# A planner's costs for overlapping steps, half-width products in P V, and matmuls into unprimed banks, in a fused attention and two-MoE kernel

## The chip, the cores and the metric

The kernel runs on one core of a Trainium2 chip. The metric is device time in microseconds, the median over runs. Engine names below: PE is TensorE (PEld its weight loads), ACT is ScalarE, DVE is VectorE, POOL is GpSimd, SP is SyncE, whose queue issues most DMAs.

## The reference

Attention with a window of 32 keys and 32 global tokens, then two feed-forward blocks, all in fp32; 2304 tokens of width 512.

```python
B, H, S, D = 4, 8, 512 + 32, 64             # 512 local and 32 global tokens
s_g = scale * q_g @ concat(k_g, k_l).T      # global queries see every key
out_g = softmax(s_g) @ concat(v_g, v_l)
s_ll = where(abs(i - j) <= 32, scale * q_l @ k_l.T, -1e9)
out_l = softmax(concat(scale * q_l @ k_g.T, s_ll)) @ concat(v_g, v_l)
x = concat(out_g, out_l)                    # 2304 x 512
h = x @ w_in                                # 512 -> 2048
y = (h * clip(h + 3, 0, 6) / 6) @ w_out     # 2048 -> 512
z = maximum(maximum(y @ w1, y @ w2), y @ w3)    # 512 -> 768
out = z @ w_out2                            # 768 -> 512
```

## The kernel before

No instruction is issued where it is written. Every function calls `op(engine, us, fn, due, r=, w=)`, which records a step with an engine (or two to choose from: `AD` is ACT or DVE, `DP` is DVE or POOL), an assumed duration, a priority and the buffers that it reads and writes. At the end `Plan.order()` runs a list scheduler over all steps: for each engine it keeps the time at which it is free (`free`), takes the ready step of least `due`, and writes the order down; the engines then run their queues in that order on the chip, and semaphores hold what is not ready. The assumed durations are constants beside each `op` (0.665 for an exponential of 224 columns, 0.47 for a row maximum) or the functions `mmt`, `act`, `dve`, `pool` of the number of columns. In `order()` a step that depends on another engine's step may start 0.12 after that one's end, a PE step's result is there `DRAIN` after its last issue, and an engine is free at the end of its step. `rel` is an earliest planned time, which holds loads back; the loads of the later weights are released `LAG` before their use.

The stages in the order of time:

- Attention, 16 pairs of heads (`pair`), four to a batch. Per pair: scores (L421, four 64x64 tiles of the PE array), row maximum with the mask added (L434, DVE), exponential (L440, ACT), guard and reciprocal (DVE or ACT), normalization (L465, POOL), transposes `flip` (L477, PE), copies out of the bank (L379, ACT or DVE) and P V (`pv`, L503): for each of four blocks i of 128 queries, two blocks of keys (kb 0 with 128 rows, kb 1 with 96), each for both heads side by side in the array. The keys stand in the order global, first 256 local, global, and so on, so that each query block sees two key blocks. Global queries have their own steps (`globals_`, L536 to L577).
- The first product x @ w_in (`first`, L643), in between the attention steps as soon as its weights are decoded (`decode`, `join`: L590 to L617) and its tokens are there. Every fp32 operand is split in a high and a low part, and three matmuls stand for one product.
- The second product (`long_`, L807), the third (`quad`, L931) and the fourth (`single` L1087, `double`) by seven block products P1 to P7 where a plain split has eight, on token groups A (256 columns), B (512) and C (320). The operands come back from DRAM (`gload`, L796), are split (L730 on ACT, L625 on DVE), and sums of banks are copied from bank to bank (`take`) so that a later product accumulates on them.

The PSUM has eight banks. In the third and fourth products `quad` uses tag `bac` for the banks that a product starts afresh and `bb` for the one into which `take` copies a partial result, on which a matmul then accumulates without a start. For this, before the third product, `prime` runs one 128x512 matmul with a start into each of the two banks of `bb` (6 and 7).

The costs as they stand before:

```python
mmt = lambda n, cols: n * (cols + 32) / 2400.0
act = lambda n: 0.18 + n * 0.00083
dve = lambda n: 0.155 + n * 0.00104
pool = lambda n: 0.08 + n * 0.0025
```

Of the kernel before, what the change touches and what calls it, by code (L numbers as in the profile page):

```python
# [20 lines left out]
B, H, SL, SG, D = 4, 8, 512, 32, 64  # L21
# [75 lines left out]
class Plan:  # L97
# [39 lines left out]
    def order(self):  # L137
# [4 lines left out]
        free, cand, out, pipe, port, form = {}, {}, [], 0.0, 0.0, "F"  # L142
# [40 lines left out]
        while len(out) < len(self.ops):  # L183
            picks, wait, at = [], {}, {}
# [15 lines left out]
            t, _, _, _, o, e = min((p for p in picks if p[0] <= t0 + WAIT), key=lambda p: p[1:4])  # L200
# [13 lines left out]
                form = FORM.get(o.what, "F")  # L214
                o.us += TURN
            o.start, o.end = t, t + o.us
            free[o.eng] = o.end
            if o.two:
                port = o.end
            if o.kb:  # L220
# [6 lines left out]
            out.append(o)  # L227
            for s in o.succ:
                s.left -= 1
                s.ready = max(s.ready, o.end if s.eng == o.eng and not o.kb else o.done + 0.12)  # L230
                if not s.left:
                    enter(s)
        return out
# [2 lines left out]
PLAN = []  # L236
WAIT = 0.02
RATE = 340.0
DRAIN = 0.18
PAIRS = 3  # L240
SPLIT = 2
WIDE = 4
TS = "BC"
STEPS = (7.2, 13, 13, 15)
LAG = 84.0
W4DUE = 4
BIAS = -0.5
SHARE = 0.0
# [8 lines left out]
def body(ctx, tc, q_n, k_n, v_r, msk, msk_g, w_in, w_o, w_3, w_4, out):  # L257
    nc = tc.nc
# [3 lines left out]
    op = plan.op  # L262
    mmt = lambda n, cols: n * (cols + 32) / 2400.0
# [62 lines left out]
    ps = Region("ps", lambda at, n: banks[at])  # L326
# [14 lines left out]
    T = {}  # L341
# [46 lines left out]
    def pair(b, pr, s0):  # L388

        S = {}  # L390
# [14 lines left out]
        for grp in (((0, 1),) if b >= PAIRS else ((0,), (1,))):  # L405
# [89 lines left out]
            def pv(grp=grp):  # L495

                for u in grp:
                    for v in range(2):
                        i = 2 * u + v
                        for kb, n in ((0, 128), (1, 96)):  # L500
                            at = (2 * v + kb) * 128
                            for hh in range(2):
                                nc.tensor.matmul(ob()[64 * hh:64 * hh + 64, 128 * i:128 * i + 128],  # L503
                                                 lhsT=V()[0:n, hh, i + kb], rhs=PTS[u][hh]()[0:n, at:at + 128],
                                                 start=(kb == 0), stop=(kb == 1))

            op("PE", 0.92 * k, pv, s1 + 7, r=[x for u in grp for x in PTS[u]] + [V], w=[(ob, u) for u in grp], what="pv")

# [325 lines left out]
    plan.event(lambda: (p1.close(), rr.open(), rf.open()), ("lp", "rx", "rq"), ("rr", "rf"))  # L834
    t = TC
    for i, (p, c, seed) in enumerate(turns):
        if i == 2:
            WO["s"] = Buf(T["wb"])
            w_sum("s", "21", "22", ALU.add, TC + 2 * LEN - 12)
            w_long("P5", "s", TC + 2 * LEN - 4)  # L840
            w_sum("s", "s", "11", ALU.subtract, TC + 3 * LEN - 18)
            w_long("P6", "s", TC + 3 * LEN - 6)
            w_sum("21", "11", "21", ALU.subtract, TC + 3 * LEN - 14)
            w_long("P7", "21", TC + 4 * LEN - 8)
            w_long("P4", "22", TC + 5 * LEN - 8)
            w_sum("12", "12", "s", ALU.subtract, TC + 5 * LEN)
            w_long("P3", "12", TC + 6 * LEN - 8)
        long_(p, c, 1e5 + t, t, seed)
        t += mmt(48, TOK[c][1])
# [53 lines left out]
    T["h2"], T["hv"] = Spot(1536, [(rf, 0), (rf, 4096)]), Spot(1536, [(rf, 2048), (rf, 5632)])  # L903
    T["u2"] = Spot(5376, [(re, 8), (re, 5384), (rr, 4104)])
    T["ot"], T["t4"] = Spot(512, places(rf, 7936, 512, 4)), Spot(512, [(rf, 9984), (rf, 3584)])
    T["bac"] = Spot(1, places(ps, 0, 1, 6))
    T["bb"] = Spot(1, places(ps, 6, 1, 2))

    def prime(R, tag, due):
        for i in range(len(T[tag].places)):  # L910
            bank = Buf(T[tag])
            op("PE", mmt(1, 512), lambda bank=bank: nc.tensor.matmul(
                bank(), lhsT=R()[:, 0:128], rhs=R()[:, 0:512], start=True, stop=True), due, r=[(R, "hi")], w=[bank],
               what="prime")

    def quad(L, R, n, es, us, o12, o22, due, k="bac", m="bb", K=2, scale=None):

# [70 lines left out]
    S["C"] = operands(yb("C"), [Y["C"]], yk("C"), "sC", TOK["C"][1], TD - 8)  # L988
    plan.event(lambda: (fw_es.close(), re.open()), ("fw",), ("re",))
    S["B"] = operands(yb("B"), [Y["B"]], yk("B"), "sB", TOK["B"][1], TD + 8)  # L990
    prime(S["A"]["P1"], "bb", 2e5)
    ORDER = [(i, c) for i, c in zip((0, 1, 0, 1, 0, 1), "AACCBB")] + [(i, c) for i in range(2, 9) for c in "CAB"]
    t = TD
    M, L3 = {}, {}
# [193 lines left out]
```

## Time and profile before

| | |
|---|---|
| median of 3 runs | 735.83 us (735.71 to 736.17) |
| the profiled execution | 737.57 us |
| its span, first to last instruction | 735.6 us |
| instructions in the span | 14020 |
| mean granted TensorE clock | 0.999 |
| PE busy | 721.7 us, 98% of the span |
| DVE, ACT, POOL busy | 559.3, 408.5, 145.5 us |
| mean DMA rate | 179 GB/s |

The profiled execution lies 1.97 us above its span and 1.74 us above the median of the timed runs. A PE that is busy is one with a matmul in its pipe; the busy time counts no slower issue.

### The profile page before, as it was taken

Reading aid. Unit: us, or ns where it says so; the run is one execution under the profiler, and the core shown is the slowest. Engines: PE = TensorE matmul, PEld = TensorE weight load, DVE = VectorE, ACT = ScalarE, POOL = GpSimd, SP = SyncE. Lnnn points to the kernel's source line nnn. Section 1 sums busy time; section 2 is a strip of 40 time slices with the busy share of each in tenths; the row PEclk is TensorE's granted clock in tenths of the full one; section 3 lists DMA queues with packets and bytes.
Section 4 is the critical chain, followed back from the end, with each engine's and each line's share of the span. In section 5 each row is a group of like instructions: output and inputs, shape, how many; then the busy total and the mean of one; then the engine's idle time right before and its main releaser. Section 6 shows DMA issues by size and latency. Waiting matters only on the chain.

```text
span 735.6 us, 14020 instructions
## 1 busy us (share of the span) xinstructions
PE 721.7 (98%) x5303; PEld 638.5 (87%) x5303; DVE 559.3 (76%) x1155; ACT 408.5 (56%) x847; POOL 145.5 (20%) x158
## 2 busy tenths in 40 slices
PE   6999999999999999999999999999999999999998
PEld 4877777888887899998898999898899989998998
DVE  5897889465858767679987769999987884487891
ACT  5887878575634354356654557574545534353462
POOL 3566778531300000001000000003200120030000
PEclk9999999999999999999999999999999999999999
DMA  8257667503538794667656769501354462346552
GB/s 296 72 170 240 228 218 268 182 1 113 218 116 293 283 373 168 222 239 238 185 148 202 206 202 300 165 1 31 120 173 148 167 208 87 101 154 198 171 172 86
DMA packets 73426, 131.70 MB, mean 179 GB/s; under 512 B 5008, under 2 KB 43920, under 8 KB 72336
## 3 DMA queue, kind: packets, MB, share of 16 engines
q1 hardware_dynamic: 73072, 130.51, 53.3%
q8 instruction: 41, 0.67, 0.4%
q10 hardware_dynamic: 288, 0.31, 0.1%
q14 instruction: 25, 0.20, 0.1%
HBM read 85.32 MB, written 45.48 MB: 178 GB/s over the span
## 4 chain that ended last, share of the span: by engine, by line
PE 88%; DMA 6%; DVE 3%; POOL 1%; issue 1%; ACT 1%; SPq 0%; DVEq 0%; ACTq 0%; POOLq 0%
PE bank L931 31%; PE bank L643 22%; PE bank L807 21%; PE o L503 3%; PE s L477 3%; DMA raw<-in_w_in_dram 2%; PE s L421 2%; PE bank L1087 2%; PE s L577 1%; PE s L536 1%; DMA raw<-in_w_dram 1%; DMA qr<-in_qn_dram 1%; DMA fw<-gsC 1%; DMA raw<-in_w_o_dram 1%; POOL rw L617 1%
## 5 line engine op out<-in xcount | busy, mean ns | idle before, releaser
L643 PE MATMUL bank<-rx,rw 128*128 128x512 f32 (+1 forms) x960 | 200.1, 363 | 1.3 <-POOL rw L617 1.0
L643 PEld LDWEIGHTS bank<-rx,rw 128*128 128x128 f32 x960 | 161.1, 188 | 28.6 <-issue 4.8
L807 PE MATMUL bank<-rr,rw 128*128 128x320 f32 (+2 forms) x912 | 154.8, 331 | 0.4 <-DVE rr L625 0.4
L807 PEld LDWEIGHTS bank<-rr,rw 128*128 128x128 f32 x912 | 140.1, 188 | 14.6 <-DVE rr L625 0.9
L931 PE MATMUL bank<-rw,rr 128*128 128x256 f32 (+2 forms) x648 | 99.9, 302 | 0.4 <-DVE rf L379 0.3
L931 PEld LDWEIGHTS bank<-rw,rr 128*128 128x128 f32 x648 | 90.3, 188 | 5.3 <-DVE rf L379 0.7
L730 ACT CAST rr<-fw 128x1024 fp32r<-128x1024 f32 (+2 forms) x76 | 62.1, 820 | 52.4 <-PE bank L807 43.3
L625 DVE TENSOR_TENSOR rr<-fw,rr 128x1024 fp32r<-128x1024 f32 (+2 forms) x76 | 70.9, 939 | 21.7 <-ACT rr L730 20.8
L465 POOL TENSOR_TENSOR tbuf<-tbuf,nm 128x448 f32<-128x448 f32 x64 | 61.7, 987 | 63.5 <-DVE nm L456 37.1
L440 ACT ACTIVATE tbuf<-tbuf,nm 128x224 f32<-128x224 f32 x128 | 60.4, 475 | 8.5 <-DVE nm L434 8.4
L653 ACT ACTIVATE rq<-bank,three 128x512 f32<-128x512 f32 (+1 forms) x60 | 38.0, 634 | 45.7 <-PE bank L643 43.2
L379 ACT COPY rf<-bank 128x512 f32<-128x512 f32 (+2 forms) x70 | 32.0, 464 | 45.5 <-PE bank L931 36.7
L655 DVE SCALAR_TENSOR_TENSOR rq<-rq,bank 128x512 f32<-128x512 f32 (+1 forms) x60 | 37.1, 618 | 26.5 <-ACT rq L653 25.9
L931 PE MATMUL bank<-re,rr 128*128 128x512 f32 x222 | 54.8, 391 | 0.0
L931 PE MATMUL bank<-rw,re 128*128 128x256 f32 (+2 forms) x369 | 53.7, 291 | 0.0
L931 PEld LDWEIGHTS bank<-rw,re 128*128 128x128 f32 x369 | 49.3, 188 | 1.4
L931 PEld LDWEIGHTS bank<-re,rr 128*128 128x128 f32 x222 | 40.8, 188 | 8.0
L1026 DVE TENSOR_TENSOR rf<-rf,bank 128x256 f32<-128x256 f32 (+2 forms) x72 | 37.4, 529 | 13.2 <-PE bank L931 12.1
L434 DVE CUSTOM_DVE_ANT_0 tbuf<-s,mask 128x224 f32<-128x224 f32 x112 | 37.8, 383 | 8.0 <-PE s L421 6.9
L625 POOL TENSOR_TENSOR rf<-rf 128x256 f32<-128x256 f32 (+2 forms) x19 | 18.9, 1002 | 110.6 <-DVE rf L625 59.5
L625 DVE TENSOR_TENSOR rf<-rf 128x256 f32<-128x256 f32 (+4 forms) x69 | 36.1, 551 | 3.8 <-DMA rf<-hd 3.1
L625 POOL TENSOR_TENSOR rq<-rq 128x256 f32<-128x256 f32 (+1 forms) x33 | 26.2, 796 | 41.5 <-DVE rq L625 37.7
(122 smaller groups left out, 1058.2 us busy)
## 6 DMA issues: line engine op xcount, KB each, us to landing
fw<-gsB SPq DMA_DIRECT2D x28, 512.0 KB, 4.5
raw<-in_w_dram SPq DMA_DIRECT2D x24, 512.0 KB, 3.9
fw<-gsC SPq DMA_DIRECT2D x28, 320.0 KB, 3.8
raw<-in_w_in_dram SPq DMA_DIRECT2D x16, 512.0 KB, 4.9
raw<-in_w_o_dram SPq DMA_DIRECT2D x16, 512.0 KB, 5.2
fw<-gsA SPq DMA_DIRECT2D x28, 256.0 KB, 3.0
gsB<-rq SPq DMA_DIRECT2D x6, 1024.0 KB, 4.3
rf<-hd SPq DMA_DIRECT2D x14, 384.0 KB, 4.6
```

The lines of the kernel that those rows point to most:

```text
L379: (nc.scalar.copy if eng == "ACT" else nc.vector.tensor_copy)(out=out, in_=in_)
L434: nc.vector.tensor_tensor_reduce(out=tb[hh]()[:, v, 0:WIN], in0=sb[hh]()[:, v * WIN:v * WIN + WIN], in1=mask()[:, i], scale=-0.125, scalar ...
L440: nc.scalar.activation(out=t, in_=t, func=ACTF.Exp, scale=-1.0, bias=nm()[:, 0, hh, v:v + 1], accum_out=nm()[:, 1, hh, v:v + 1])
L465: nc.gpsimd.tensor_tensor(out=t, in0=t, in1=r, op=ALU.mult)
L625: ENG[e].tensor_tensor(out=out, in0=a, in1=b, op=f)
L643: nc.tensor.matmul(ps()[:, 0:m], lhsT=w[:, i, k], rhs=xs(c)[:, j, k], start=(k == 0 and s == 0), stop=(k == KC - 1 and s == 2))
L653: op("ACT", us, lambda ps=ps, m=m, out=out: nc.scalar.activation(out=out(), in_=ps()[:, 0:m], func=ACTF.Relu, bias=three), -100, r=[ps], w ...
L655: op("DVE", us, lambda ps=ps, m=m, out=out: nc.vector.scalar_tensor_tensor(out=out(), in0=out(), scalar=6.0, in1=ps()[:, 0:m], op0=ALU.min ...
L730: op("ACT", act(n) + 0.01, lambda: nc.scalar.copy(out=out(0), in_=src()), due, r=r, w=[(w, "hi")], what=what + "_hi")
L807: nc.tensor.matmul(A[e]()[:, 0:n], lhsT=w[:, 2 * fp + f, u, e], rhs=r[:, v, f], start=(seed is None and fp + f + s == 0), stop=(fp == 3 an ...
L931: nc.tensor.matmul(bank()[:, 0:n], lhsT=w[:, u, k], rhs=r[:, v, k], start=(start and k + s == 0), stop=(k == K - 1 and s == 2), skip_group ...
L1026: op("DVE", dve(n), lambda q=q, src=src, mv=mv: nc.vector.tensor_tensor(out=mv(q)(), in0=mv(q)(), in1=src(), op=ALU.max), -200, r=[bank], ...
```

## The change

Four things. In `order()` an engine is free again before the end of its step: by `LAP`, which is 0.1 for ACT, 0.08 for DVE, 0.04 for POOL, 0.2 for an exponential and 0.155 for a row maximum (each has a second, short instruction that reads the accumulator). The hop between engines is 0.05 where it was 0.12, and `DRAIN` 0.165 where it was 0.18; `LAG` grows from 84 to 95. The chip runs no other instruction for this, but nearly every queue has another order. Second, P V: in query block 0 the second key block is multiplied for queries 64 to 127 alone (the first 64 queries have a window that ends before it, and their weights there are zero). Third, `prime` and its two matmuls are gone: `bb` lies in the two banks that the last P4 product of group B used with all 512 columns, and `bac` in the six others, those first that are free first. Fourth, for that the last chain of the second product takes the next two banks in turn, by four unused `Buf`.

```diff
@@ -214,7 +214,7 @@
                 form = FORM.get(o.what, "F")
                 o.us += TURN
             o.start, o.end = t, t + o.us
-            free[o.eng] = o.end
+            free[o.eng] = o.end - LAP.get(o.what, LAP.get(o.eng, 0.0))
             if o.two:
                 port = o.end
             if o.kb:
@@ -227,7 +227,7 @@
             out.append(o)
             for s in o.succ:
                 s.left -= 1
-                s.ready = max(s.ready, o.end if s.eng == o.eng and not o.kb else o.done + 0.12)
+                s.ready = max(s.ready, o.end if s.eng == o.eng and not o.kb else o.done + HOP)
                 if not s.left:
                     enter(s)
         return out
@@ -236,13 +236,16 @@
 PLAN = []
 WAIT = 0.02
 RATE = 340.0
-DRAIN = 0.18
+DRAIN = 0.165
+
+LAP = dict(ACT=0.1, DVE=0.08, POOL=0.04, exp=0.2, rowmax=0.155, g_exp=0.2, g_rowmax=0.155)
+HOP = 0.05
 PAIRS = 3
 SPLIT = 2
 WIDE = 4
 TS = "BC"
 STEPS = (7.2, 13, 13, 15)
-LAG = 84.0
+LAG = 95.0
 W4DUE = 4
 BIAS = -0.5
 SHARE = 0.0
@@ -499,10 +502,11 @@
                         i = 2 * u + v
                         for kb, n in ((0, 128), (1, 96)):
                             at = (2 * v + kb) * 128
+                            q = 64 if kb and not i else 0
                             for hh in range(2):
-                                nc.tensor.matmul(ob()[64 * hh:64 * hh + 64, 128 * i:128 * i + 128],
-                                                 lhsT=V()[0:n, hh, i + kb], rhs=PTS[u][hh]()[0:n, at:at + 128],
-                                                 start=(kb == 0), stop=(kb == 1))
+                                nc.tensor.matmul(ob()[64 * hh:64 * hh + 64, 128 * i + q:128 * i + 128],
+                                                 lhsT=V()[0:n, hh, i + kb], rhs=PTS[u][hh]()[0:n, at + q:at + 128],
+                                                 start=(kb == 0), stop=(kb == 1), skip_group_check=True)
 
             op("PE", 0.92 * k, pv, s1 + 7, r=[x for u in grp for x in PTS[u]] + [V], w=[(ob, u) for u in grp], what="pv")
 
@@ -834,6 +838,9 @@
     plan.event(lambda: (p1.close(), rr.open(), rf.open()), ("lp", "rx", "rq"), ("rr", "rf"))
     t = TC
     for i, (p, c, seed) in enumerate(turns):
+        if i == len(turns) - 1:
+            whole = [bank.at for bank in chain["B"]]
+            skipped = [Buf(T["bank"]) for _ in range(4)]
         if i == 2:
             WO["s"] = Buf(T["wb"])
             w_sum("s", "21", "22", ALU.add, TC + 2 * LEN - 12)
@@ -903,15 +910,12 @@
     T["h2"], T["hv"] = Spot(1536, [(rf, 0), (rf, 4096)]), Spot(1536, [(rf, 2048), (rf, 5632)])
     T["u2"] = Spot(5376, [(re, 8), (re, 5384), (rr, 4104)])
     T["ot"], T["t4"] = Spot(512, places(rf, 7936, 512, 4)), Spot(512, [(rf, 9984), (rf, 3584)])
-    T["bac"] = Spot(1, places(ps, 0, 1, 6))
-    T["bb"] = Spot(1, places(ps, 6, 1, 2))
-
-    def prime(R, tag, due):
-        for i in range(len(T[tag].places)):
-            bank = Buf(T[tag])
-            op("PE", mmt(1, 512), lambda bank=bank: nc.tensor.matmul(
-                bank(), lhsT=R()[:, 0:128], rhs=R()[:, 0:512], start=True, stop=True), due, r=[(R, "hi")], w=[bank],
-               what="prime")
+
+
+    assert all(wide[at] == 512 for at in whole)
+    left = [[bank.at for bank in chain[c]] for c in "CB"]
+    early = [at for at in range(8) if at not in whole + left[0] + left[1]]
+    T["bac"], T["bb"] = Spot(1, [(ps, at) for at in early + left[0] + left[1]]), Spot(1, [(ps, at) for at in whole])
 
     def quad(L, R, n, es, us, o12, o22, due, k="bac", m="bb", K=2, scale=None):
 
@@ -988,7 +992,6 @@
     S["C"] = operands(yb("C"), [Y["C"]], yk("C"), "sC", TOK["C"][1], TD - 8)
     plan.event(lambda: (fw_es.close(), re.open()), ("fw",), ("re",))
     S["B"] = operands(yb("B"), [Y["B"]], yk("B"), "sB", TOK["B"][1], TD + 8)
-    prime(S["A"]["P1"], "bb", 2e5)
     ORDER = [(i, c) for i, c in zip((0, 1, 0, 1, 0, 1), "AACCBB")] + [(i, c) for i in range(2, 9) for c in "CAB"]
     t = TD
     M, L3 = {}, {}
```

The built programs differ as follows. On DVE the number of instructions grows from 1157 to 1175, on ACT it falls from 715 to 710 and on POOL from 163 to 150 (of the third product's weight sums with 256 columns, POOL has 8 where it had 17). On PE two are gone, and 32 of the 256 P V matmuls have 64 columns (each is two instructions in the trace, one for each half of an fp32 operand). Line numbers of the changed kernel are 3 to 4 higher.

At the head of the program, PE's order in the first pairs; in the rows, `tbuf` holds the weights of softmax, `s_` and `bank_` are PSUM banks, `o` is the output bank of P V. Before, from the global scores of the first two pairs:

```order
L536 MATMUL s_130<-kr,qr 64x304 x2
L536 MATMUL s_126<-kr,qr 64x304 x2
L421 MATMUL bank_100<-kr,qr 64x160
...
L421 MATMUL bank_101<-kr,qr 64x128
L477 MATMUL s_127<-ident,tbuf_108 128x128 x4
L477 MATMUL s_128<-ident,tbuf_110 128x128 x4
L503 MATMUL o<-pt,vr 64x128 x8
L477 MATMUL s_129<-ident,tbuf_112 128x128 x4
L477 MATMUL s_130<-ident,tbuf_114 128x128 x4
L421 MATMUL s_126<-kr,qr 64x128
```

There P V of the first half (`L503`, eight matmuls) follows directly on that half's transposes. The same place in the changed kernel, where L540, L480, L424 and L507 are the lines of global scores, transposes, scores and P V:

```order
L540 MATMUL s_130<-kr,qr 64x304 x2
L540 MATMUL s_126<-kr,qr 64x304 x2
L480 MATMUL s_127<-ident,tbuf_108 128x128 x4
L480 MATMUL s_128<-ident,tbuf_110 128x128 x4
L424 MATMUL s_129<-kr,qr 64x128
...
L424 MATMUL s_130<-kr,qr 64x224
L480 MATMUL s_126<-ident,tbuf_112 128x128 x4
L480 MATMUL s_127<-ident,tbuf_114 128x128 x4
L507 MATMUL o<-pt,vr 64x128 x2
L507 MATMUL o<-pt,vr 64x64 x2
L507 MATMUL o<-pt,vr 64x128 x12
```

The scores of the second pair's other half come before the global scores; between the first transposes (into s_127 and s_128) and the first P V there now stand eight score matmuls of the third pair and eight more transposes, and P V of both halves runs as one block of 16, of which two have 64 columns.

At the passage from the second product (L807) to the third (L931), PE's order before, with the two primes (L912):

```order
L807 MATMUL bank_2573<-rr,rw 128x512 x3
L912 MATMUL bank_100<-rw 128x512
L912 MATMUL bank_101<-rw 128x512
L931 MATMUL bank_2568<-rw,rr 128x256 x6
L931 MATMUL bank_2569<-rw,rr 128x256 x6
L931 MATMUL bank_100<-rw,rr 128x256 x6
...
L931 MATMUL bank_2568<-rw,rr 128x320 x6
L807 MATMUL bank_2572<-rr,rw 128x512 x3
```

The primes write the banks 100 and 101, which are 6 and 7; seven block products follow before the next L807. And in the changed kernel, where L811 and L935 are the same lines:

```order
L811 MATMUL bank_2580<-rr,rw 128x512 x3
L935 MATMUL bank_100<-rw,rr 128x256 x6
L935 MATMUL bank_101<-rw,rr 128x256 x6
L935 MATMUL bank_2583<-rw,rr 128x256 x6
L935 MATMUL bank_100<-rw,rr 128x256 x6
L811 MATMUL bank_2579<-rr,rw 128x512 x3
L811 MATMUL bank_2580<-rr,rw 128x512 x3
L811 MATMUL bank_2579<-rr,rw 128x512 x3
L811 MATMUL bank_2580<-rr,rw 128x512 x3
L935 MATMUL bank_2583<-rw,rr 128x256 x6
```

The primes are gone; the third product begins with four block products where seven stood, then come the last four rows of the second product.

On SP's queue, the loads of the last part of the second product before (L796 loads operands of groups A, C and B, L722 the raw third weights, 512 KB each):

```order
L796 DMA fw<-gsA 128x2x256 x8
L722 DMA raw<-in_w_dram 128x1024 x2
L796 DMA fw<-gsC 128x2x320 x4
L722 DMA raw<-in_w_dram 128x1024
L796 DMA fw<-gsC 128x2x320 x4
```

All eight loads of group A stand before the weights. And in the changed kernel:

```order
L800 DMA fw<-gsA 128x2x256 x7
L726 DMA raw<-in_w_dram 128x1024 x2
L800 DMA fw<-gsA 128x2x256
L800 DMA fw<-gsC 128x2x320 x4
L726 DMA raw<-in_w_dram 128x1024
L800 DMA fw<-gsC 128x2x320 x4
```

The first two loads of third weights have moved ahead of the last load of group A.

## Rows read from the trace of the kernel before

**Rows 1.** The page: busy us of each engine, share of the span, instructions.

```profile
PE 721.7 (98%) x5303; PEld 638.5 (87%) x5303; DVE 559.3 (76%) x1155; ACT 408.5 (56%) x847; POOL 145.5 (20%) x158
```

**Rows 2.** Windows by stage: us, busy and count by engine, clock, DMA share, GB/s.

```profile
3.80:38.00 34.20, 30.78 (x413) 23.09 (x413) 27.13 (x124) 26.76 (x90) 15.41 (x17) 1.00 0.53 183
38.00:222.00 184.00, 181.47 (x1717) 145.01 (x1711) 133.92 (x390) 126.53 (x352) 93.07 (x96) 1.00 0.51 176
222.00:478.00 256.00, 255.31 (x1539) 235.22 (x1539) 202.83 (x319) 134.66 (x208) 7.24 (x5) 1.00 0.69 231
478.00:667.00 189.00, 188.58 (x1144) 172.15 (x1143) 150.34 (x259) 89.99 (x155) 27.30 (x25) 1.00 0.38 122
667.00:733.00 66.00, 65.53 (x500) 63.02 (x498) 44.97 (x66) 29.25 (x44) 1.02 (x1) 1.00 0.48 151
```

**Rows 3.** PE's waits, by line and releaser: us in total, times, longest.

```profile
PE s L421 <- DMA kr<-in_kn_dram: 3.8, 1, 3.8
PE bank L421 <- DMA qr<-in_qn_dram: 2.1, 1, 2.1
PE bank L643 <- POOL rw L617: 1.0, 1, 1.0
PE s L421 <- ACT rw L616: 1.0, 1, 1.0
PE o L503 <- DVE pt L379: 0.8, 2, 0.6
PE s L477 <- POOL tbuf L465: 0.8, 2, 0.5
PE bank L807 <- DVE rr L625: 0.4, 1, 0.4
```

**Rows 4.** Order of time, PE: a whole P V and a global P V.

```profile
83.54 1.96 PE L503 MATMUL o<-pt,vr 128*64 128x128 f32 x32
...
137.12 1.31 PE L577 MATMUL s<-pt,vr 128*64 128x32 f32 x40
```

**Rows 5.** The chain that ended last: start, us, what (primes; first product around scores).

```profile
93.62 0.71 PE bank L643 x3
94.33 0.76 PE s L421 x16
95.08 0.91 PE bank L643 x3
...
477.80 0.46 PE bank L912 x2
```

**Rows 6.** Order of time near the first P V.

```profile
14.55 0.69 DVE L379 COPY pt<-s 128x512 f32<-128x512 f32 x1
...
15.29 1.09 PE L503 MATMUL o<-pt,vr 128*64 128x128 f32 x14 [0.63 <-DVE pt L379]
```

**Rows 7.** The chain ahead of PE's wait at 443.7 us.

```profile
436.05 0.42 SPq L722
436.57 5.82 DMA fw<-gsC
442.47 0.74 ACT rr L730
```

**Rows 8.** Order of time: row maxima on DVE, exponentials on ACT, each followed directly.

```profile
32.22 0.39 DVE L434 CUSTOM_DVE_ANT_0 tbuf<-s,mask 128x224 f32<-128x224 f32 x1
32.53 0.08 DVE L434 DVE_READ_ACCUMULATOR2_ANT nm<- 128x1 f32 x1
32.53 0.39 DVE L434 CUSTOM_DVE_ANT_0 tbuf<-s,mask 128x224 f32<-128x224 f32 x1
...
48.60 0.48 ACT L440 ACTIVATE tbuf<-tbuf,nm 128x224 f32<-128x224 f32 x1
48.97 0.20 ACT L440 ACTIVATION_READ_ACCUMULATOR tbuf<-tbuf,nm 128x1 f32 x1
49.06 0.48 ACT L440 ACTIVATE tbuf<-tbuf,nm 128x224 f32<-128x224 f32 x1
```

**Rows 9.** Groups by form, 0 to 215 us: two DVE steps of the weight decoding.

```profile
L600 DVE SCALAR_TENSOR_TENSOR rq<-raw,rq 128x512 int32<-128x512 int32 x16 | 14.0, 873 | 0.4
...
L592 DVE TENSOR_SCALAR raw<-raw 128x512 int32<-128x512 int32 x16 | 11.1, 692 | 6.7 <-DMA raw<-in_w_in_dram 6.7
```

**Rows 10.** The same two lines in order of time, one of each.

```profile
83.37 0.69 DVE L600 SCALAR_TENSOR_TENSOR rq<-raw,rq 128x512 int32<-128x512 int32 x1
...
85.13 0.43 DVE L592 TENSOR_SCALAR raw<-raw 128x512 int32<-128x512 int32 x1 [1.08 <-DMA raw<-in_w_in_dram]
```

## The prediction

> **What bounds the kernel now.** I read the page first: PE is busy for 721.7 of 735.6 us, and no other engine above 76% [rows 1]. Then the windows by stage, because an average hides where PE can still gain. From 38 us to the end of the matmuls PE idles for 2.53, 0.69, 0.42 and 0.47 us in four stages (window less busy), and for 3.42 us in the stretch 3.8 to 38 us [rows 2]. Third, PE's own waits: after the two for the first DMAs (3.8 and 2.1 us) there are eleven: 1.0, 1.0, twice two that sum to 0.8, and 0.4 [rows 3], and four more of 0.2 to 0.3, together 4.9 us. So PE's queue sets the time. A change can win by giving PE less to issue, or by removing from these 4.9 us; no order can win much more. What it can lose has no such limit.
>
> **The sum.** The rows come from the profiled execution, 737.57 us with a span of 735.6; the median of the runs shown is 735.83. All terms are differences, and I set them against the median.
>
> P V with 64 columns. The trace has no P V of 64 columns; it has 128 and, in the global P V, 32, with the same 64-column weights for two heads side by side [rows 4]. With two heads side by side, the 32 instructions of a whole P V are 16 slots in 1.96 us, 0.123 each; the 40 of the global one are 20 slots in 1.31 us, 0.066 each. Halving the columns would halve 0.123 to 0.061, which is under the 0.066 that a slot of 32 columns takes anyway: so at best 0.066, a gain of 0.057. A straight line between the two rows gives 0.085 at 64 columns, a gain of 0.038. The change halves two slots per pair (one for each half of an fp32 operand), 32 in all: 1.2 to 1.8 us of PE time. The first five pairs run before 38 us, where PE also waits for others, and may give nothing: 0.8 as the lower bound. I take 1.3.
>
> The Trainium skill speaks against this term: "TensorE: Matmul & The Clock Gate", section "Wait — 56ns, not 53.3ns?", says that without hardware decoding the sequencer spends about 62 ns on each MATMUL, which becomes the bound for short ones. By it a slot of two could not fall below 0.124 us and the term would be 0. The trace disagrees: 40 instructions in 1.31 us are 0.033 each [rows 4].
>
> The primes are 0.46 us of PE's queue with the full array and nothing beside them [rows 5]; they lie in a stage in which PE is busy throughout, so all 0.46 comes back. Their cover for a first accumulation is replaced by what P4 of group B leaves in its banks; that costs no instruction.
>
> Changes of the array's shape. Scores, P V and full matmuls use the array in three shapes. The trace shows a price: three matmuls of the first product take 0.71 us behind transposes, which use the full array, and 0.91 behind scores [rows 5], 0.20 for a return. In PE's order I count 78 such changes before and 71 after; before the first block of long products both orders have 21, so all seven lie where PE is the bound. A return costs 0.2, a change between two tiled shapes may cost nothing; at 0.1 each they give 0.7 (0 to 1.4).
>
> The new order's waits. At two of the three places shown I can say which way it goes. At the first P V, PE waited 0.63 us for a copy on DVE that began at 14.55, while the transposes it copies had been issued before [rows 6]; most of the 0.8 of that line. In the new order eight scores (0.76 for sixteen instructions, [rows 5]) and eight transposes stand between, so the copy is covered: about -0.7. At the last part of the second product, PE waited 0.4 us at 443.7 for the first operand of group C, whose load took 5.82 us because it was issued at 436.57, right behind two raw weight loads of 512 KB [rows 3, 7]. In the new order those two go ahead of the last load of group A. C's load then has less in front of it, but A's last load has more: it landed 3 us after its issue and would now take up to 5.8, which eats the time that it had in hand. I take 0.2 of the 0.4.
>
> For the other 3.7 us, what counts is whether the plan's figures are true. By rows they are nearer than before: successive row maxima start 0.31 apart (32.22, 32.53), successive exponentials 0.46 apart (48.60, 49.06) [rows 8]. The plan reckoned with 0.47 and 0.665 and now with 0.47 - 0.155 = 0.315 and 0.665 - 0.2 = 0.465. DVE's copy ended at 15.24 and PE started at 15.29 [rows 6], the new hop of 0.05 where the plan had 0.12. An exponential that is planned 0.2 too long, 128 times, puts up to 26 us of ACT time into the plan that is not there, so attention was planned late and product steps pulled ahead. The new order takes attention when it is really ready. What this does for the remaining waits no row tells; the ends are all gone (-3.7) and as many new ones as now (+3.7, the nearest row being the 1.0 us of a single wait). I take -1.0, since the figures that decide them are now within 0.01 us of the rows. In sum waits give -0.7 - 0.2 - 1.0 = -1.9.
>
> Sum: -1.3 - 0.5 - 0.7 - 1.9 = -4.4, so 735.8 - 4.4 = **731.4 us**. The least favourable ends give -0.8 - 0.5 - 0 + 3.7 = +2.4, 738.2; the best -1.8 - 0.5 - 1.4 - 4.9 = -8.6, 727.2.
>
> The cover. Thirteen steps leave POOL, DVE gets 18 more instructions; at the 0.43 of the shorter decoding step [rows 10] they are 8 us. In 478 to 667 us DVE is busy for 150 of 189 us [rows 2]; 8 us more stay hidden there as long as no `take` stands behind them. `LAG` lets raw weights in 11 us earlier; they meet loads that PE does not wait for, except at the place at 443 us.
>
> **Rivals.**
>
> *VectorE falls behind (slower).* The plan now frees DVE 0.08 before each end, but while GpSimd works some DVE steps last longer: the two decoding steps have means of 873 and 692 ns in the attention stage [rows 9] where single ones take 0.69 and 0.43 [rows 10]. That is 0.18 and 0.26 us on 16 each, 7 us; similar losses on the other steps can double it. The old surplus in the plan covered this; without it, the planned order is ahead of DVE, and PE, in order, waits at the copies and gates. If half of 14 us reaches PE, the time is 735.8 - 2.5 (the first three terms) + 7 = 740.3. It decides from 2.5 us of new waits on. Against it: POOL and ACT keep reserves in the plan, and DVE idles for 50 of 184 us there [rows 2].
>
> The Trainium skill would make this rival general: "VectorE: DVE Perf Modes", section "The DRAIN you can't avoid", says that the next operation does not start until the pipe is empty. By it no LAP would be true for DVE, and the plan would be wrong at every step. The trace disagrees: a row maximum of 0.39 us is followed after 0.31 [rows 8].
>
> *No change.* Waits of the kind shown come back at other places, 2 to 3 us of them, and eat the first three terms: 735 us, between 734.4 and 737.3.
>
> *The order was the brake.* All waits behind the first loads vanish and the shape changes cost their full price: 728.5 us. For it: the waits that I could follow go away. Against it: part of them end on DMAs, which the plan knows no better than before.
>
> *The edit of P V does nothing*, because slots are bound by the weight loads: then 732.7, inside the forecast.
>
> **How the numbers follow.** Forecast (730 to 734.3) 0.60; order as the brake, below 730, 0.14; no change 0.15; VectorE behind 0.11. What a measurement of this kernel can tell from no change is about 0.2%, 1.5 us. Faster by more is 0.60 + 0.14 = 0.74, within 0.15, slower 0.11. For 8 times in 10 I leave out some 0.06 below 728.0 and 0.12 above 736.5. The likeliest case alone spans 730 to 734.3.
>
> **What would show it.** Right: P V of a pair (32 instructions) about 0.1 us shorter; no L912; the wait of P V for DVE at 15 us gone; PE busy near 718 to 719 us in a span near 731; PE idle in 38 to 222 us no more than 2.5 us. Wrong: PE waits for DVE or POOL in 40 to 200 us above 5 us in sum; waits for a `take` (L379) in 478 to 667 us, where PE now idles for 0.4 us; a wait for group A's last operand at 442 us.

## The result and the profile after

The change is slower: 742.73 us median against 735.80 for the kernel before, each from six runs on one chip; ratio 1.0093, 95% interval 1.0076 to 1.0109. The profiled execution took 742.68 us with a span of 740.9. The forecast was 731.4, with a range from 728.0 to 736.5.

The page of the changed kernel, its first part: busy time, share of the span, instructions.

```profile
PE 723.6 (98%) x5301; PEld 641.2 (87%) x5301; DVE 565.2 (76%) x1173; ACT 403.1 (54%) x842; POOL 130.6 (18%) x145
```

PE is busy for 1.9 us more than before [rows 1], with less to do. In two stretches of this execution the granted clock was 0.50 (1.2 GHz), behind the stalls at 86 and 684 us that are shown below (columns as in [rows 2], the clock third from last):

```profile
86.10:89.40 3.30, 3.30 (x12) 2.26 (x10) 3.30 (x9) 3.30 (x12) 3.22 (x4) 0.50 0.65 225
686.80:690.20 3.40, 3.40 (x18) 3.40 (x17) 2.64 (x4) 2.08 (x2) 0.00 (x0) 0.50 0.67 191
```

Matmuls of 256 columns start 0.213 us apart in the second stretch and 0.117 behind it; the two stretches together are worth an estimated 3.4 us of PE time, half their length. The windows by stage, against [rows 2] (the last one is 7 us longer here):

```profile
3.80:38.00 34.20, 33.52 (x423) 25.14 (x424) 31.92 (x129) 30.67 (x106) 18.83 (x19) 1.00 0.57 196
38.00:222.00 184.00, 180.45 (x1718) 146.26 (x1717) 131.02 (x386) 123.94 (x339) 89.06 (x94) 0.99 0.52 179
222.00:478.00 256.00, 253.57 (x1536) 233.90 (x1535) 202.53 (x325) 128.63 (x199) 4.00 (x3) 1.00 0.69 226
478.00:667.00 189.00, 187.15 (x1126) 170.26 (x1126) 154.78 (x268) 88.89 (x154) 14.98 (x13) 1.00 0.37 122
667.00:740.00 73.00, 68.83 (x505) 65.57 (x503) 44.77 (x65) 29.64 (x46) 2.23 (x2) 0.98 0.44 141
```

PE's idle time (window less busy) fell from 3.42 to 0.68 us ahead of 38 us, and grew from 2.53 to 3.55, from 0.69 to 2.43 and from 0.42 to 1.85 in the next three. The last matmul of the first product (L643, now L647) starts at 314.06 before and 310.23 after: 3.8 us ahead. The last matmul of all starts at 732.25 and 737.52: 5.3 us behind. Not all of this is the change's: the kernel before with the edit of P V alone, every queue in the old order (it is among the experiments), starts the same two matmuls at 309.90 and 730.24. So the new order is no earlier at the end of the first product than the old one can be, and from there to the last matmul it takes 427.3 us where P V alone takes 420.3. These are single executions; by them the 7 us that the change lost lie behind the first product. PE's waits, against [rows 3]:

```profile
PE s L424 <- DMA kr<-in_kn_dram: 3.9, 2, 3.8
PE s L480 <- DVE nm L437: 1.9, 1, 1.9
PE bank L935 <- DVE rr L629: 1.5, 1, 1.5
PE bank L811 <- DVE rr L629: 1.5, 3, 0.7
PE bank L647 <- DVE rq L659: 1.1, 1, 1.1
PE bank L935 <- DVE re L629: 1.1, 1, 1.1
PE bank L935 <- ACT re L1112: 0.9, 1, 0.9
PE bank L811 <- ACT rr L734: 0.9, 2, 0.6
```

L811 is the second product, L935 the third and fourth; L629 and L734 make their operands' low and high parts. In the kernel before, the same products (L807, L931) waited 0.4, 0.3 and 0.2 us. Behind the first loads the waits sum to 9.9 us, against 4.9 before. Four places are followed here; the others of a microsecond are at 105 us (1.1, L647) and 336 us (0.6 and 0.45).

At 86 us, the longest of them, in the order of time:

```profile
81.03 1.17 POOL L468 TENSOR_TENSOR tbuf<-tbuf,nm 128x448 f32<-128x448 f32 x1
81.33 1.15 DVE L596 TENSOR_SCALAR raw<-raw 128x512 int32<-128x512 int32 x1
82.16 0.92 POOL L629 TENSOR_TENSOR rq<-rq 128x256 f32<-128x256 f32 x1
82.59 1.04 DVE L601 SCALAR_TENSOR_TENSOR rq<-rq,raw 128x512 int32<-128x512 int32 x1
85.90 0.97 PE L480 MATMUL s<-ident,tbuf 128*128 128x128 f32 x4 [1.93 <-DVE nm L437]
```

Two decoding steps on DVE run beside GpSimd's and take 1.15 and 1.04 us, where such steps take 0.43 [rows 10] and 0.69 (332.09 us) alone; the row maxima for which PE's transposes wait stand behind them on DVE.

At 440 us, the chain of work that ended last (start, us, what):

```profile
432.73 6.46 DMA fw<-gsA
...
439.27 0.63 ACT rr L734
...
439.92 0.70 DVE rr L629
...
440.67 1.44 PE bank L811 x10
```

This is the load of group A's last operand behind the raw weights that were moved ahead of it: 6.46 us, and PE stands 0.6 us (0.26 and 0.34) around it. P V alone, in the old order, stands 1.4 us at the same place:

```profile
441.07 0.42 PE L808 MATMUL bank<-rr,rw 128*128 128x320 f32 x1 [0.97 <-ACT rr L731]
441.93 1.29 PE L808 MATMUL bank<-rr,rw 128*128 128x320 f32 x7 [0.44 <-DVE rr L626]
```

So this place is no cost of the new order.

At 488 us, single instructions of L629 in 484 to 489 us (engine, operation, count: shortest, median and longest ns, first and last start):

```profile
L629 DVE TENSOR_TENSOR rr<-rf,rr x2: 812/1914/3016, 484.6 to 485.3; 128x640 fp32r<-128x640 f32 x2
L629 POOL TENSOR_TENSOR re<-rf,re x1: 2667/2667/2667, 485.0 to 485.0; 128x1024 fp32r<-128x1024 f32 x1
```

Two equal subtractions on DVE take 0.81 and 3.02 us. The second meets GpSimd's of 1024 columns, begun 0.3 us before it, and ends 0.7 us after that one's end. PE stands 1.5 us, until 490.29, for DVE's next operand (the expectations below call it 1.8). The program's own plan shows that the two were never meant to meet. Three of its steps, with their names written out (start, end and time at which the operands are ready, us on the plan's clock):

```
POOL  r_lo of group B, 1024 columns   495.990  498.630  ready 480.130
PE    P1 of tokens 0 and 128          675.216  676.296  ready 675.204
PE    P6 of tokens 1664 and 1792      676.296  677.376  ready 675.254
```

The plan keeps GpSimd and DVE apart (`port` in `order()`), and places GpSimd's step at 496. But GpSimd has nothing else in its queue, and the chip starts it when its operands are there. PE runs 4.9 us behind the plan here, so 496 would be 501 on the chip; it started at 485.02.

At 683 us, the order of time on all engines:

```profile
674.34 2.05 SPq L1066 DMA_DIRECT2D out_dram<-rf  x4
676.48 1.22 SPq L1102 DMA_DIRECT2D rf<-hd  x2
678.21 2.09 DVE L629 TENSOR_TENSOR rf<-rf 128x384 f32<-128x384 f32 x4 [3.23 <-DMA rf<-hd]
683.09 1.50 DVE L629 TENSOR_TENSOR rf<-rf 128x384 f32<-128x384 f32 x3 [2.79 <-DMA rf<-hd]
683.14 1.15 ACT L1112 CAST re<-rf 128x1152 fp32r<-128x1152 f32 x1 [5.28 <-DMA rf<-hd]
684.35 0.51 PE L935 MATMUL bank<-rw,re 128*128 128x256 f32 x2 [0.91 <-ACT re L1112]
685.91 1.37 PE L935 MATMUL bank<-rw,re 128*128 128x256 f32 x8 [1.06 <-DVE re L629]
```

Four small stores of the global rows hold SP's queue for 2.05 us, where the plan has 0.7; the two loads of tokens 0 and 128 are issued behind them and land after 5.3 and 6.0 us, where the plan has 4.0 and 4.7. PE stands in front of their product, which the plan put ahead of P6 because P6 would have been ready 0.04 us after the start of that product. The low clock behind this stall (0.95 in the mean over 667 to 700 us) is about 1.6 us more in this execution, while its other runs had mean clocks of 0.998 to 1.0.

### The profile page after: what moved, and what is told of

It reads as the page before. It is cut to its first block, busy times and chain, and to the rows that moved or that the text cites. A ratio compares the mean times of both kernels' runs of the same rounds, so it can differ in the third digit from the quotient of the medians.

```text
span 740.9 us, 13990 instructions
## 1 busy us (share of the span) xinstructions
PE 723.6 (98%) x5301; PEld 641.2 (87%) x5301; DVE 565.2 (76%) x1173; ACT 403.1 (54%) x842; POOL 130.6 (18%) x145
## 4 chain that ended last, share of the span: by engine, by line
PE 77%; DVE 9%; DMA 7%; ACT 2%; POOL 2%; issue 2%; SPq 1%; ACTq 0%; DVEq 0%; POOLq 0%
PE bank L935 29%; PE bank L647 23%; PE bank L811 17%; PE o L507 2%; PE s L480 2%; DVE tbuf L437 2%; PE s L424 2%; DMA rf<-hd 2%; DMA raw<-in_w_in_dram 1%; DVE rr L629 1%; PE s L581 1%; DMA gsC<-fw 1%; DMA fw<-gsA 1%; POOL rq L629 1%; DMA raw<-in_w_dram 1%
## 5 line engine op out<-in xcount | busy, mean ns | idle before, releaser
L647 PE MATMUL bank<-rx,rw 128*128 128x512 f32 (+1 forms) x960 | 199.3, 364 | 1.1 <-DVE rq L659 1.1
L647 PEld LDWEIGHTS bank<-rx,rw 128*128 128x128 f32 x960 | 162.4, 189 | 26.4 <-issue 3.9
L811 PE MATMUL bank<-rr,rw 128*128 128x320 f32 (+2 forms) x912 | 155.3, 331 | 2.4 <-DVE rr L629 1.5
L811 PEld LDWEIGHTS bank<-rr,rw 128*128 128x128 f32 x912 | 140.4, 188 | 16.6 <-DVE rr L629 2.2
L935 PE MATMUL bank<-rw,rr 128*128 128x256 f32 (+2 forms) x648 | 100.0, 303 | 1.9 <-DVE rr L629 1.5
L935 PEld LDWEIGHTS bank<-rw,rr 128*128 128x128 f32 x648 | 90.1, 188 | 7.5 <-DVE rr L629 1.7
L734 ACT CAST rr<-fw 128x1024 fp32r<-128x1024 f32 (+2 forms) x76 | 61.9, 820 | 52.9 <-PE bank L811 40.3
L629 DVE TENSOR_TENSOR rr<-fw,rr 128x1024 fp32r<-128x1024 f32 (+2 forms) x76 | 70.6, 935 | 21.8 <-ACT rr L734 20.9
L935 PE MATMUL bank<-rw,re 128*128 128x256 f32 (+2 forms) x369 | 55.3, 296 | 2.0 <-DVE re L629 1.1
L935 PE MATMUL bank<-re,rr 128*128 128x512 f32 x222 | 54.2, 390 | 0.0
L935 PEld LDWEIGHTS bank<-rw,re 128*128 128x128 f32 x369 | 50.2, 192 | 4.0 <-DVE re L629 1.3
L382 ACT COPY rf<-bank 128x256 f32<-128x256 f32 (+2 forms) x71 | 32.3, 462 | 36.0 <-PE bank L935 31.6
L629 DVE TENSOR_TENSOR rf<-rf 128x256 f32<-128x256 f32 (+4 forms) x78 | 41.2, 554 | 9.2 <-DMA rf<-hd 8.6
L935 PEld LDWEIGHTS bank<-re,rr 128*128 128x128 f32 x222 | 41.0, 188 | 8.1
L1029 DVE TENSOR_TENSOR rf<-rf,bank 128x256 f32<-128x256 f32 (+2 forms) x72 | 36.7, 528 | 11.7 <-PE bank L935 10.7
L629 POOL TENSOR_TENSOR rq<-rq 128x256 f32<-128x256 f32 (+1 forms) x33 | 25.8, 784 | 83.7 <-DVE rq L629 81.4
L480 PEld LDWEIGHTS s<-ident,tbuf 128*128 128x128 f32 x256 | 28.8, 141 | 8.4 <-issue 5.7
```

Source lines behind the costliest of these rows:

```text
L480: nc.tensor.transpose(FB[u][hh]()[:, at:at + 128], TB[u][hh]()[:, v, kb * 128:kb * 128 + 128], ident)
L629: ENG[e].tensor_tensor(out=out, in0=a, in1=b, op=f)
L647: nc.tensor.matmul(ps()[:, 0:m], lhsT=w[:, i, k], rhs=xs(c)[:, j, k], start=(k == 0 and s == 0), stop=(k == KC - 1 and s == 2))
L734: op("ACT", act(n) + 0.01, lambda: nc.scalar.copy(out=out(0), in_=src()), due, r=r, w=[(w, "hi")], what=what + "_hi")
L811: nc.tensor.matmul(A[e]()[:, 0:n], lhsT=w[:, 2 * fp + f, u, e], rhs=r[:, v, f], start=(seed is None and fp + f + s == 0), stop=(fp == 3 an ...
L935: nc.tensor.matmul(bank()[:, 0:n], lhsT=w[:, u, k], rhs=r[:, v, k], start=(start and k + s == 0), stop=(k == K - 1 and s == 2), skip_group ...
```

## The experiments

Each run was timed in five rounds beside the kernel before; the ratio is to that kernel. One hundredth is 7.4 us.

**Which part costs.** All old figures on the changed kernel:

```diff
-DRAIN = 0.165
+DRAIN = 0.18
-LAP = dict(ACT=0.1, DVE=0.08, POOL=0.04, exp=0.2, rowmax=0.155, g_exp=0.2, g_rowmax=0.155)
-HOP = 0.05
+LAP = {}
+HOP = 0.12
-LAG = 95.0
+LAG = 84.0
```

> The changed kernel with the plan's old figures (no LAP, HOP 0.12, DRAIN 0.18, LAG 84): only P V with 64 columns, no primes and the new banks are left of the change. Theory A, the plan's new figures cost it all: the two edits give back their PE time, about 2 us, 733 to 734.5. Theory B, LAG alone: the same. Theory C, the banks of the double products cost it: 740 or more. PE's last work of the second product then ends no later than before (485.7 us).

738.65 us, 1.0024 (1.0003 to 1.0044). Some 5 us of the loss hang on the figures, but what is left is not faster.

The kernel before with the new figures alone (P V whole, primes as before):

> The kernel before with LAP, HOP 0.05, DRAIN 0.165 and LAG 95 alone; P V whole and primes as before. Theory A: 743 to 745, because the loss stays and the 2 us of the two edits are missing. Theory B: the same. Theory C: 734 to 737.

742.63, 1.0086 (1.0060 to 1.0112). The figures carry nearly all of the loss.

The changed kernel with `LAG = 84.0`:

> The changed kernel with LAG back at 84. Theory B, raw weight loads let in 11 us earlier push other loads back: 734 to 737, and the waits at 336 and 440 us are gone. Theory A: 740 to 743, with new waits between 335 and 345 and at 488 and 683 us staying.

743.19, 1.0100 (1.0071 to 1.0129). The wait at 440 us went, and the time did not: LAG is not the cause. In the new plan the steps from the second product on stand 8 to 14 us earlier, so 95 lets raw weights in at about the same point of the work as 84 did before; my "11 us earlier" was wrong.

`LAP` reduced to exponentials and row maxima:

> The changed kernel with LAP only for the exponentials and row maxima; the three figures for whole engines (ACT 0.1, DVE 0.08, POOL 0.04) are gone, HOP, DRAIN and LAG stay new. Theory A in its narrow form, the figures for whole engines take away the reserve that the operand splits on ACT, DVE and POOL need from 330 us on: 732 to 736, with less than 3 us of PE waits behind 330 us. Theory A in its wide form (HOP, or any denser order): 740 or more. Theory C: 740 or more.

742.15, 1.0080 (1.0051 to 1.0108). The narrow theory fell.

`LAP = {}` with the new HOP and DRAIN:

> The changed kernel without LAP; HOP 0.05 and DRAIN 0.165 stay. Theory of the reserve (every figure that brings the plan's ready times forward takes away time that loads and operand splits need in reality, whichever it is): slower than the version with all old figures, 738.65, and faster than the change, 742.7: 739.5 to 742. Rival, the overlaps alone do the harm: 738 to 739.

742.22, 1.0059 (1.0039 to 1.0079). Without `LAP` more than half of the loss stays. Neither `LAG` nor `LAP` alone is to blame; `HOP` and `DRAIN` were not taken out by themselves.

The edit of P V alone (the `q` of the diff on the kernel before; the order of every engine is that of before):

> The kernel before with the edit of P V alone; every engine's order is that of before. The prediction's own term (1.3 us, 0.8 to 1.8 of PE time): matmuls of P V 1.6 us less busy and 734 to 735. Rival, the saved PE time is given back in waits on operands that do not come earlier: 736 +- 0.7, with PE's waits up by as much as its busy time falls.

735.78, 0.9983 (0.9965 to 1.0001). A whole P V in the order of time, against the 1.96 of [rows 4]:

```profile
80.89 1.86 PE L504 MATMUL o<-pt,vr 128*64 128x128 f32 x32
```

The saved 0.10 us is there in 15 of the 18 stretches of P V and sums to 1.5 us; the time fell by about 1.2 by the ratio, whose interval just reaches no change, so the rival isn't ruled out.

No primes and the new banks alone:

> The kernel before with no primes and the new banks of the double products alone; P V is whole, the plan's figures are the old ones. The prediction's term: 0.46 us less, 735.5. Rival, that the first double products now wait for banks which the second product holds: 737 to 739, with 1 to 3 us of new PE waits between 470 and 500 us.

740.29, 1.0044 (1.0026 to 1.0063). By the ratio (some 3 us) the rival's size is met, and its mechanism is not. In the order of time around the new wait:

```profile
489.57 3.02 POOL L628 TENSOR_TENSOR re<-rf,re 128x1024 fp32r<-128x1024 f32 x1
490.26 0.41 DVE L382 COPY rf<-bank 128x256 f32<-128x256 f32 x1
490.60 2.67 DVE L628 TENSOR_TENSOR rf<-rf 128x640 f32<-128x640 f32 x1
493.19 0.95 DVE L628 TENSOR_TENSOR re<-rf,re 128x768 fp32r<-128x768 f32 x1
494.20 0.50 PE L934 MATMUL bank<-rw,re 128*128 128x256 f32 x2 [1.64 <-DVE re L628]
```

It is a low part of group B again: planned at 500, its operands ready at 491, run at 489.57 though PE is nowhere more than 1.4 us off the plan there. DVE's 0.82 lasts 2.67, and PE waits. In the kernel before, all of group B's low parts run on DVE. The banks only moved the plan to an order with this step on GpSimd.

**The early GpSimd step.** One instruction more, every engine's order kept: GpSimd first copies one column of what the last `take` in the plan has written.

```diff
+    if e == "POOL" and n == 512:
+        nc.gpsimd.tensor_copy(out=hold, in_=taken[-1])
     tt(e, o(1), v(i), o(0).bitcast(F32), ALU.subtract)
```

On the version with all old figures:

> The version with all old figures (P V with 64 columns, no primes, new banks), every engine in the same order, with one instruction more: ahead of each low part of group B's operands that GpSimd makes, GpSimd copies one column of what the last take in the plan has written, so that it can't begin before the time that the plan gave it. Theory G: there the low part of 1024 columns began some 10 us ahead of its planned time and stopped VectorE for 2 us where PE waits; 735 to 736.5, PE's wait of 1.6 us at 487 us gone. Rival, the banks cost it in another way: 738 to 739.

736.17, 0.9995 (0.9981 to 1.0010): 2 us gone with one instruction. The wait of 1.6 us is gone.

On the changed kernel:

> The changed kernel with the same one instruction, every engine's order kept. Theory G: the stall of 1.8 us at 488 us goes, 740 to 741.5, and the tail stays as it is. Rival: GpSimd's low part only moves and stops VectorE later, 742 to 743.

742.29, 1.0071 (1.0053 to 1.0090). The medians say 0.4 us, the ratios 1.6; the intervals overlap. The trace shows the stall gone; the three subtractions behind the place of the long one, in the order of time:

```profile
484.78 0.82 DVE L630 TENSOR_TENSOR rr<-rf,rr 128x640 fp32r<-128x640 f32 x1
485.51 0.82 DVE L630 TENSOR_TENSOR rf<-rf 128x640 f32<-128x640 f32 x1
486.25 1.22 DVE L630 TENSOR_TENSOR rr<-rf,rr 128x1024 fp32r<-128x1024 f32 x1
```

GpSimd's step now begins at 498.55 and stops DVE there for as long (2.98 us for one step), where PE loses less: 0.7 us at 502 us. So the rival is right in part.

**The late loads.** The store of the global rows planned at what it takes:

```diff
-        op("SP", 0.7, store, due, ...
+        op("SP", 0.7 if t0 < B * SL else 2.2, store, due, ...
```

> The changed kernel with one figure more: the store of the global rows, four transfers that hold SP's queue for 2.1 us where the plan has 0.7, is planned with 2.2. The plan then takes the product of tokens 0 and 128 later. Theory: the stall of 2.5 us at 683 us and the low clock behind it (1.6 us) go; 738 to 739.5. Rival, the stall only moves to the next product whose loads are late: 741 or more.

741.61, 1.0053 (1.0035 to 1.0071). Better by the ratio, but the rival was right too: PE's longest wait of the tail is now 1.8 us for a `take` (L382). DVE in the order of time:

```profile
678.14 2.09 DVE L629 TENSOR_TENSOR rf<-rf 128x384 f32<-128x384 f32 x4 [3.34 <-DMA rf<-hd]
682.82 0.56 DVE L629 TENSOR_TENSOR rf<-rf 128x384 f32<-128x384 f32 x1 [2.58 <-DMA rf<-hd]
683.29 0.68 DVE L386 TENSOR_SCALAR rf<-bank 128x512 f32<-128x512 f32 x1
683.89 0.55 DVE L629 TENSOR_TENSOR rf<-rf 128x384 f32<-128x384 f32 x1
684.36 0.43 DVE L382 COPY bank<-bank 128x256 f32<-128x256 f32 x1
```

DVE stands 2.58 us in front of a sum whose load is late, and the copy that PE needs is behind it. So with the loads' and row stores' own time as well:

```diff
-                o.end = pipe + 1.8
+                o.end = pipe + (3.2 if o.what in ("hload", "hstore") else 1.8)
```

> The changed kernel with the store of the global rows planned at 2.2 us, as in the run before, and the loads and stores of the tail's rows planned 1.4 us longer (3.2 behind the transfer, where the plan has 1.8). Theory T, VectorE stands behind sums whose loads come later than planned, and PE's copies stand behind them: 737.5 to 739.5, with less than 2 us lost between 666 us and the end. Rival, the tail loses because ready times are planned without reserve on every step: 740.5 to 742.

737.42, 1.0007 (0.9988 to 1.0025): the two figures of the DMA plan give back 6 us. They also draw a new order from 645 us of the plan on, so part of it can be the draw. In 667 to 700 us PE has no idle time, where the change had 1.96 and half speed for a while:

```profile
667.00:700.00 33.00, 33.00 (x230) 30.81 (x230) 26.46 (x40) 14.83 (x20) 0.00 (x0) 1.00 0.67 206
```

Both mends together on the changed kernel:

> The two together on the changed kernel. If both theories hold and add up: 736 to 738, against 742.7 for the change. If the order with the new figures has a loss of another kind: 740 or more.

736.57, 0.9995 (0.9982 to 1.0008). Then the hold ahead of every GpSimd step that the plan starts more than 3 us after its operands are ready:

```diff
+            if o.may and o.eng == "POOL" and o.start - o.ready > 3 and taken:
+                nc.gpsimd.tensor_copy(out=hold, in_=taken[-1])
             o.fn(o.eng) if o.may else o.fn()
```

> The changed kernel with the tail's figures (store 2.2, loads 3.2) and the one-column copy ahead of every GpSimd step that the plan starts more than 3 us after its operands are ready: group B's low part, and a weight sum of 512 columns that the plan has at 348 us and that ran at 335 us. Theory G: the stall of 1.4 us at 336 us goes too, 734.8 to 736 against 736.6 without this hold. Rival, that stall has another cause: 736 to 737.5.

736.16, 0.9983 (0.9967 to 0.9998): clearly faster than the change, and just clear of the kernel before. Whether this last hold did anything the run can't tell (0.9995 and 0.9983 overlap). The same mends with the old figures:

> The version with all old figures (P V with 64 columns, no primes, new banks) with both mends: the hold on GpSimd and the tail's figures. If the banks have no cost but the early low part: 734.5 to 735.5, 0.4 or so below P V alone. If they have another: 736 or more.

736.63, 1.0002 (0.9985 to 1.0019), no better than with the first hold alone (0.9995). By its expectation this speaks for another cost of the banks; its interval overlaps that of P V alone (0.9983), and it stays open.

**Reserve, or one order among many.** P V alone on the kernel before, with only the hop of the plan changed:

```diff
-    s.ready = max(s.ready, o.end if s.eng == o.eng and not o.kb else o.done + 0.12)
+    s.ready = max(s.ready, o.end if s.eng == o.eng and not o.kb else o.done + 0.2)
```

> The kernel before with P V of 64 columns (735.8) and HOP 0.2 in place of 0.12, which plans every handover later and so with more reserve. Theory R, the reserve in the figures is what kept the order good: 735 to 736.5. Theory L, the order of before is a lucky one and any other figure makes another order with stalls of its own: 737 to 741.

738.67, 1.0022 (1.0003 to 1.0042). And with 0.13:

> The same with HOP 0.13, a change of a hundredth of a microsecond that no row could tell from 0.12. Theory R: 735 to 736.5. Theory L: 737 to 741, in other places than with 0.2.

742.96, 1.0077 (1.0047 to 1.0108), against 0.9983 for 0.12. A hundredth of a microsecond in one figure of the plan costs as much as the whole change. Its waits, by line and releaser, are short and spread over the program (442, 453, 472, 489, 658 and 666 us among others; the one at 442 us stands in P V alone too):

```profile
PE bank L808 <- DVE rr L626: 1.4, 4, 0.4
PE o L504 <- DVE pt L379: 1.3, 3, 0.6
PE bank L808 <- ACT rr L731: 1.2, 2, 1.0
PE bank L932 <- ACT bank L379: 1.0, 1, 1.0
PE s L421 <- DVE g L541: 1.0, 1, 1.0
```

Theory R is out: 0.13 plans later than 0.12, not earlier. Theory L fits. The order with 0.13 and both mends:

> P V of 64 columns on the kernel before with HOP 0.13 (743.0), now with the tail's figures (store 2.2, loads 3.2) and the hold on GpSimd steps that the plan starts over 3 us after their operands. If the two faults are what any other order meets: 736 to 738. If that order's stalls (at 442, 453, 472, 489, 658 and 666 us) have other causes: 740 or more, with only the loss behind 680 us smaller.

740.28, 1.0070 (1.0047 to 1.0093). The mends end the idle time behind 667 us and do not save this order; why its other stalls come is open. The mended changed kernel with HOP 0.06:

> The changed kernel with both mends (736.2) and HOP 0.06 in place of 0.05: another order by a hundredth. If the mended plan bears small changes: 735 to 737.5. If the order stays a matter of luck: 738 to 742.

734.84, 0.9985 (0.9967 to 1.0002). This order differs from that of 0.05 in most places on VectorE, ScalarE and GpSimd, and keeps the time. In the stage that cost the change 1.85 us PE idles for 0.15:

```profile
478.00:667.00 189.00, 188.85 (x1135) 172.28 (x1134) 155.01 (x273) 87.67 (x149) 20.13 (x17) 1.00 0.37 124
```

## Why the prediction was wrong

The step that failed is "For the other 3.7 us ... I take -1.0, since the figures that decide them are now within 0.01 us of the rows." From the first product's last matmul to the last of all it takes 418.2 us before (314.06 to 732.25) and 427.3 after (310.23 to 737.52): 9 us more, and 7 more than P V alone (420.3), where I had taken 1 us less for these waits in the whole program. I had compared the figures that the change touches with rows, and taken this for the truth of the plan. What cost the time, as far as the runs show it, is where the plan is wrong elsewhere: a DMA that it ends 1.3 us too early, a store that it books at a third of its time, a GpSimd step that it starts on a clock the chip does not have. Plan and chip, read against each other: before, the second product starts 1.8 us ahead of its plan (planned 316.0, run 314.2) and the last block product 6.7 ahead; after, 2.6 behind and 11.7 behind. The new figures made the plan 13 us shorter and the chip 5 us slower.

Point by point. P V: 0.10 us per pair, as foreseen, and about 1.2 us of the time against the 1.3 taken. Primes: L912 is gone, and its 0.46 with it, but "that costs no instruction" was no proof of no cost; the edit alone made 1.0044, of which the hold on one GpSimd step gave back some 2 us; with that step held, 0.9995 against 0.9983 for P V alone, the 0.46 isn't seen. Shape changes (-0.7): not seen; P V alone ends the first product at 309.90 in the old order, the change at 310.23, and executions of one order differ there by 2 us. The first P V's wait of 0.8 for DVE is gone, as foreseen. At the place at 443 us the other sign came, the wait for group A's last operand that I had listed under wrong; its load took 6.46 us where I feared 5.8, and PE lost 0.6 us there where it had lost 0.4. PE's idle time in 38 to 222 us is 3.55, not below 2.5. My range left out this end because I bounded new waits by 3.7, the size of those that were there; nothing in the profile of before bounds them, as my first paragraph says itself ("What it can lose has no such limit").

The rivals. VectorE falling behind (740.3, one in ten) is nearest in time and half right. GpSimd does stop VectorE, and at 82 us at the decoding steps of attention, as the rival has it: PE waits 1.9 us there. But this wait stays (2.0 us) in the mended kernel of 736.16, so it is not what the mends give back. What the hold gives back is the stop at one operand of the third product: some 2 us with the old figures, 1.6 of the 7 by the ratios with the new ones, where the intervals overlap. The Trainium skill has the part that I needed: "SBUF — State Buffer", section "Who interferes with whom", says that a VectorE instruction with two inputs in SBUF contends with a GpSimd one that reads SBUF, since its second input comes through the read interface that the two share, and calls the shared pair of ports an exclusive lock. The trace agrees: 3.02 for 0.81.

The prediction sets the rule of the pipe that must be empty against [rows 8]. The Trainium skill, "VectorE: DVE Perf Modes", section "The DRAIN you can't avoid", adds to this rule that a next operation that is not held starts earlier. So a row maximum that starts after 0.31 us doesn't contradict that section.

What stays open: why the order of HOP 0.13 is slow, and a part of the 6 us between the change and its mended tail. Of these the profiles show 1.5 ahead of 657 us, where every queue has the same order, and 4.8 behind, of which 1.6 are the low clock of one execution.

## What to carry to other kernels

A planner that fixes the order can lose by its worst figure what it gains by its best: before making one figure exact, compare planned with measured start times along the whole program, and mend the largest gap first (here loads and stores on SP, then GpSimd). A step that the plan holds back by time alone starts early on the chip if its queue is empty; give it a dependence at the place that is meant. And when a change reorders everything, its forecast needs the spread of orders: one neutral change of a figure, run on the chip, showed here that it is at least 0.9%.

## What the runs showed of the hardware

A GpSimd subtraction of 1024 columns with both inputs in SBUF takes 2.41 us where no such VectorE subtraction is running when it begins (498.55 us with the hold on the changed kernel). It takes 2.67, 3.02 and 3.26 us where one still has 0.41, 0.77 and 0.99 us to run (the changed kernel, the banks alone, the hold on the old figures): 2.26 us and that rest. A VectorE subtraction with both inputs in SBUF that starts inside one makes no headway until it ends: it ends 0.68 us after it (640 columns, 0.82 alone) and 1.1 after it (1024 columns, 1.22 alone). A shift of 512 columns with a single input is stopped too (L595 in the kernel with the banks alone: 1.80 us beside a GpSimd step of 1.65, 0.41 alone). VectorE's copies out of PSUM in the same stretches keep their time (0.41 for 256 columns at 490.26 us). Four stores of 64 KB hold SP's queue for 2.05 us in sum, and loads of 384 KB issued behind them land after 5.3 and 6.0 us, where two at 673 us, ahead of them, took 3.8 and 4.5. That the stores are the reason is not shown: in the kernel before, two such loads at 661 us take 5.3 and 5.9 us with no such stores ahead, and one right behind the four stores, at 683 us, takes 4.2.
